# Attention beside a gated mlp on one core: row maxima in visits of four over six banks, and another order of the first transfers

## The chip, the cores and the metric

The kernel runs on one core of a Trainium2 chip. The metric is the device time of one execution in microseconds (us); lower is better. Before the change it is 1117.92 us, the median of three runs (1117.37 to 1118.45).

PE is TensorE (matmuls; PEld its loads of stationary operands), DVE is VectorE, ACT is ScalarE, POOL is GpSimd, SP is SyncE, which here issues most DMAs. PSUM, where matmuls write, has eight banks of 128 x 512 fp32.

## The reference

One input x of 2048 tokens x 448 feeds two branches, which a gate per token mixes: attention with 16 heads of 28, and an mlp behind a layernorm.

```python
def _A_ref(x, wqkv, wo):
    qkv = (x @ wqkv).reshape(B, S, 3, H, Dh).transpose(2, 0, 3, 1, 4)
    q, k, v = qkv[0], qkv[1], qkv[2]
    scores = einsum("bhqd,bhkd->bhqk", q, k) * (Dh ** -0.5)
    o = einsum("bhqk,bhkd->bhqd", softmax(scores), v)
    return o.transpose(0, 2, 1, 3).reshape(B, S, D) @ wo
def _B_ref(x, w1, b1, w2, b2):
    h = gelu(layernorm(x) @ w1 + b1)        # 448 -> 1792
    return h @ w2 + b2                      # 1792 -> 448
g = sigmoid((x * gate_w).sum(-1, keepdims=True))
return g * _A_ref(x, wqkv, wo) + (1 - g) * _B_ref(x, w1, b1, w2, b2)
```

All of it is fp32. The kernel splits operands into a high part that TensorE takes (type fp32r) and the low rest, and adds the products high x high, high x low and low x high: three matmuls for one product.

## The kernel before, in words

**Stages.** (1) The head: q and k of the first 512 tokens, then q, k and v of all tokens, with the layernorm's statistics beside them. (2) The mlp, in four chunks of 512 tokens; for each chunk `mlp1` makes 14 blocks of 128 hidden units (11 matmuls each, L612), and `mlp2` makes four blocks of 128 tokens (14 x 3 matmuls each, L625, L626, L630). (3) Attention: scores, exponentials on ACT, products with v, and the output projection.

**Row maxima.** The softmax needs the maximum of each row of scores ahead of the exponentials. The class `RowMax` finds it with a cheaper product of high parts: one matmul (L440) gives the scores of 128 queries of one head with 512 keys in one bank, and DVE reduces it (L420 for one bank, L422 for two neighbouring banks at once). A head has 28 rows, so four heads lie in the four strips of 32 partitions (`j`), and the heads go round by turns. A block is four heads x 512 queries: 64 such matmuls, and a 65th slot (`close`, L406) that transposes the block's maxima, eight matmuls into the next block. There are 16 blocks, 1040 slots in all. Slot and block order: `left` holds what a block has left, `done` counts slots.

**Visits.** During the mlp these slots are put between its matmuls. After each matmul of the mlp `Filler.run` adds a weight to `slot`; `due` says how many of 482 slots (`MLP_MAX`) should be done by now, spread evenly over the stretch that begins at f = 4 of the first chunk (`FS`, L667), where a matmul of `mlp1` counts 0.65 x 0.233, later 0.233, and one of `mlp2` 0.205 (`W1`, `W2`). Is a visit's worth due (`MG` = 6), then six slots are issued at once, into banks 2 to 7; banks 0 and 1 belong to the mlp. Matmuls run in the order of the program. A matmul into a bank waits until DVE has reduced what stood there; DVE takes its instructions in the order in which they stand. In the attention stage `scores` puts single slots between its own products (banks 5 and 6).

The keys for the row maxima (`khr`, four strips) are loaded by four DMAs on POOL's queue at f = 1 of the first chunk (`load_khr`, L503), the queries (`qd`) on SP's.

**The head.** `WARM` = 8 matmuls of zeros (L276) run first. q and k together have seven blocks of 128 outputs (m), and 448 inputs are laid out as four pieces of 128 rows (t; the last holds 64 rows twice). `turns` gives the order in which weights `("w", m)`, all four t at once, and inputs `("x", t)` of the first 512 tokens are fetched: w0, x0, w1, x1, w2, x2, w3, x3, w4, w5, w6; x0 on ACT's queue, all else on SP's. In the same order ACT makes the high parts (L183, L202), POOL or DVE the low parts (L184, L204), and PE runs every product that has just become possible into seven banks (L322, 77 matmuls), the products with low weights one turn later. After that come the v tiles (L234) and the other q, k tiles (L222).

Of the kernel before, what the change touches and what calls it, by code (L numbers as in the profile page):

```python
# [15 lines left out]
P = 128  # L16
# [16 lines left out]
MG = 6  # L33
FS = 4
WARM = 8
# [7 lines left out]
def kernel(ctx: ExitStack, tc: tile.TileContext, xt, wqk, wv, wo, xk, w1, b1, w2, b2,  # L43
# [114 lines left out]
    with tc.tile_pool(name="qx", bufs=2) as qx, tc.tile_pool(name="qo", bufs=4) as qo, \  # L158
# [15 lines left out]
        wh, wl, wt = {}, {}, {}  # L174

        def fetch_wqk(m):
            wt[m] = halves.pop(0).rearrange("p (t x) -> p t x", t=4)
            nc.sync.dma_start(wt[m], wqk[m])

        def split_wqk(m):  # L180
            wh[m] = qw.tile([P, 4, P], F32R, name=f"wh{m}")
            wl[m] = qw.tile([P, 4, P], F32R, name=f"wl{m}")
            nc.scalar.activation(wh[m], wt[m], AF.Copy)  # L183
            nc.gpsimd.tensor_sub(wl[m], wt[m], wh[m].bitcast(F32))  # L184
# [30 lines left out]
        def qk_tile(c, m):  # L215
            ps = next_ps()
            ops = []
            for t in range(3):
                ops += [(wh[m][:, t], xh[c][:, t]), (wh[m][:, t], xl[c][:, t]), (wl[m][:, t], xh[c][:, t])]
            ops += [(wh[m][:, 3], xh[c][:, 3]), (wl[m][:, 3], xh[c][:, 3])]  # L220
            for i, (a, b) in enumerate(ops):
                nc.tensor.matmul(ps, a, b, start=(i == 0), stop=(i == len(ops) - 1))  # L222
            qk_out(c, m, ps)
# [49 lines left out]
        zeros = spare(NF - 1)[:, 0, :P]  # L273
# [9 lines left out]
        halves = [x[:, i] for n in range(NF // 2, NF - 1) for x in [spare(n)] for i in range(2)]  # L283
        turns = [x for i in range(NM) for x in ([("w", i), ("x", i)] if i < 4 else [("w", i)])]
        for what, i in turns:
            if what == "w":
                fetch_wqk(i)
            else:
                fetch_x(0, i, nc.sync if i else nc.scalar)
# [6 lines left out]
        for v in vt:  # L296
            nc.gpsimd.memset(v[:, :, DH:DH + 1], 1.0)
            nc.gpsimd.memset(v[:, :, DH + 1:32], 0.0)
        banks = [next_ps() for m in range(NM)]
        there, pieces, late, count = [], [], [], [0] * NM  # L300
        for what, i in turns:
            if what == "w":
                if i < 4:
                    split_wqk(i)
                there.append(i)
                new = [(i, t) for t in pieces]
            else:
                split_x(0, i)
                pieces.append(i)
                new = [(m, i) for m in there]  # L310
            ops = [("hh", m, t) for m, t in new]

            low, late = late + [("lh", m, t) for m, t in new], []
            if what == "w":
                late = [x for x in low if x[1] == i]
            ops += [x for x in low if x not in late]
            ops += [("hl", m, t) for m, t in new if t < 3]
            if i == NM - 1:
                ops += late
            for k, m, t in ops:  # L320
                a, b = wl[m] if k == "lh" else wh[m], xl[0] if k == "hl" else xh[0]
                nc.tensor.matmul(banks[m], a[:, t], b[:, t], start=(count[m] == 0), stop=(count[m] == 10))  # L322
                count[m] += 1
                if m == 0 and count[m] == 11:

                    for n in range(4, NM):
                        split_wqk(n)
                    for n in range(4):
                        nc.scalar.activation(wvh[:, n], wvr[n], AF.Copy)
                        nc.gpsimd.tensor_sub(wvl[:, n], wvr[n], wvh[:, n].bitcast(F32))  # L330
# [630 lines left out]
```

## Time and profile before

| what | value |
| --- | --- |
| median of three runs | 1117.92 us |
| the profiled execution's own time | 1117.1 us |
| its span, first to last instruction | 1115.3 us |
| PE busy | 1106.8 us, 99% of the span |
| DVE / ACT / POOL busy | 741.2 / 634.8 / 334.0 us |
| first and last matmul of L322 | 6.36 us, and the first v tile starts at 26.08 us |
| first matmul of the mlp | 116.19 us |
| last visit of the mlp over | 456.98 us |

The profile is one execution. Times are us from the start of the span unless marked ns. In the order of time a row gives start, length, engine, line, operation, what it writes <- reads, the shape and how many equal instructions it joins; in brackets stands the idle time ahead of it and what ended it. In the groups of instructions the columns are the count, the busy time, the mean length in ns, then the idle time ahead and what ended it. Matmuls are pipelined: one starts before the one ahead of it has ended, so their lengths overlap, and a pace is read from starts. In the view of stretches the columns are the window, its length, the busy time of PE, PEld, DVE, ACT and POOL with the number of instructions, the granted clock of PE, the DMA engines' share and GB/s.

### The profile page before, as it was taken

Reading aid. Unit: us, or ns where it says so; the run is one execution under the profiler, and the core shown is the slowest. Engines: PE = TensorE matmul, PEld = TensorE weight load, DVE = VectorE, ACT = ScalarE, POOL = GpSimd, SP = SyncE. Lnnn points to the kernel's source line nnn. Section 1 sums busy time; section 2 is a strip of 40 time slices with the busy share of each in tenths; the row PEclk is TensorE's granted clock in tenths of the full one; section 3 lists DMA queues with packets and bytes.
Section 4 is the critical chain, followed back from the end, with each engine's and each line's share of the span. In section 5 each row is a group of like instructions: output and inputs, shape, how many; then the busy total and the mean of one; then the engine's idle time right before and its main releaser. Section 6 shows DMA issues by size and latency. Waiting matters only on the chain.

```text
span 1115.3 us, 19794 instructions
## 1 busy us (share of the span) xinstructions
PE 1106.8 (99%) x8152; PEld 674.9 (61%) x8152; DVE 741.2 (66%) x1030; ACT 634.8 (57%) x660; POOL 334.0 (30%) x354
## 2 busy tenths in 40 slices
PE   9999999999999999999999999999999999999998
PEld 7888777777777777744444444444444444454546
DVE  4553398988888889576766766666667767746103
ACT  5334651330231232287887887887878878847572
POOL 5016664242344231013112221320223024342350
PEclk9999999999999999999999999999999999999999
DMA  7988641011121023162100220012021003002011
GB/s 247 363 266 284 179 122 53 9 47 36 50 55 37 25 53 87 41 166 79 28 19 20 61 72 19 21 28 52 26 59 37 18 20 94 12 26 69 34 53 58
DMA packets 53079, 84.35 MB, mean 76 GB/s; under 512 B 8516, under 2 KB 28500, under 8 KB 52076
## 3 DMA queue, kind: packets, MB, share of 16 engines
q1 hardware_dynamic: 48588, 76.01, 22.2%
q0 software_dynamic: 4256, 6.81, 2.3%
q8 instruction: 64, 1.05, 0.4%
q10 hardware_dynamic: 144, 0.26, 0.1%
q14 instruction: 27, 0.22, 0.1%
HBM read 56.40 MB, written 26.49 MB: 74 GB/s over the span
## 4 chain that ended last, share of the span: by engine, by line
PE 98%; DVE 1%; ACT 1%; DMA 0%; issue 0%; ACTq 0%
PE bank L828 22%; PE bank L563 20%; PE bank L440 16%; PE bank L612 13%; PE bank L222 5%; PE bank L630 5%; PE bank L625 4%; PE bank L626 4%; PE bank L234 3%; PE bank L322 2%; PE bank L733 1%; PE bank L734 1%; PE bank L735 1%; DMA w1f<-in_wqk 0%; ACT khi L567 0%
## 5 line engine op out<-in xcount | busy, mean ns | idle before, releaser
L567 ACT ACTIVATE pt<-bank 128x1536 f32<-128x1536 f32 (+1 forms) x386 | 460.3, 1243 | 121.7 <-PE bank L563 121.7
L420 DVE TENSOR_REDUCE mx<-bank 128x1 f32<-128x512 f32 x618 | 409.8, 688 | 174.0 <-PE bank L440 160.1
L828 PE MATMUL bank<-pt,vg 128*32 128x512 f32 x1942 | 260.4, 602 | 0.0
L422 DVE TENSOR_REDUCE mx<-bank 128x2 f32<-128x1024 f32 x203 | 238.9, 1220 | 30.3 <-PE bank L440 30.0
L440 PE MATMUL bank<-khi,qd 28*128 28x512 f32 x512 | 241.9, 480 | 0.1
L440 PEld LDWEIGHTS bank<-khi,qd 28*128 28x128 f32 x512 | 92.3, 181 | 148.1 <-DVE mx L420 104.4
L563 PE MATMUL bank<-qh,klo 28*128 28x512 f32 x1024 | 174.2, 394 | 0.0
L563 PE MATMUL bank<-qh,khi 29*128 29x512 f32 x768 | 156.3, 480 | 0.8 <-ACT khi L567 0.6
L612 PE MATMUL bank<-y,w1f 128*128 128x512 f32 x616 | 151.9, 397 | 0.0
L612 PEld LDWEIGHTS bank<-y,w1f 128*128 128x128 f32 x616 | 112.6, 188 | 33.1 <-issue 10.8
L563 PE MATMUL bank<-ql,khi 28*128 28x512 f32 x768 | 128.8, 390 | 0.0
L617 POOL TENSOR_TENSOR hl<-h,hh 128x512 fp32r<-128x512 f32 x56 | 72.5, 1295 | 117.6 <-ACT h L616 77.4
L615 ACT ACTIVATE hh<-bank,b1s 128x512 fp32r<-128x512 f32 x56 | 38.7, 691 | 98.6 <-PE bank L612 98.6
L828 PEld LDWEIGHTS bank<-pt,vg 128*32 128x32 f32 x1942 | 44.6, 108 | 78.7 <-issue 78.3
L563 PEld LDWEIGHTS bank<-qh,klo 28*128 28x128 f32 x1024 | 87.2, 185 | 3.6
L636 ACT ACTIVATE h<-bank 128x448 f32<-128x448 f32 x16 | 8.7, 546 | 137.9 <-PE bank L630 103.6
L749 POOL DMA_DIRECT2D lt<-ob x15 | 10.9, 727 | 253.0 <-DVE ob L748 253.0
L630 PE MATMUL bank<-w2h,hl 128*128 128x448 f32 x224 | 85.0, 379 | 0.0
L563 PEld LDWEIGHTS bank<-qh,khi 29*128 29x128 f32 x768 | 60.6, 181 | 39.8 <-ACT pt L567 25.0
L625 PE MATMUL bank<-w2h,hh 128*128 128x448 f32 x224 | 83.3, 372 | 0.0
L626 PE MATMUL bank<-w2l,hh 128*128 128x448 f32 x224 | 81.9, 366 | 0.0
L440 PE MATMUL bank<-khr,qd 28*128 28x512 f32 x512 | 80.3, 467 | 0.5 <-issue 0.3
(135 smaller groups left out, 1298.0 us busy)
## 6 DMA issues: line engine op xcount, KB each, us to landing
qk<-hl SPq DMA_DIRECT2D x28, 512.0 KB
vs<-vt SPq DMA_DIRECT2D x16, 256.0 KB
s<-in_xt SPq DMA_DIRECT2D x16, 256.0 KB
raw<-in_xt SPq DMA_DIRECT2D x15, 256.0 KB
rc<-rls POOLq DMA_DIRECT2D x60, 64.0 KB, 2.2
w1f<-in_xk SPq DMA_DIRECT2D x8, 448.0 KB
gbs<-h SPq DMA_DIRECT2D x16, 224.0 KB
klo<-qk SPq DMA_DIRECT2D x16, 224.0 KB
```

The lines of the kernel that those rows point to most:

```text
L222: nc.tensor.matmul(ps, a, b, start=(i == 0), stop=(i == len(ops) - 1))
L420: nc.vector.reduce_max(self.mx[:, c0:c0 + 1], bank[:, b0], axis=AX)
L422: nc.vector.reduce_max(self.mx[:, c0:c1 + 1:c1 - c0], bank[:, b0:b1 + 1], axis=AX)
L440: nc.tensor.matmul(bank[:, b], self.qds[self.n][r, i * P:(i + 1) * P], khi[self.n // NC][r, k * 512:(k + 1) * 512], start=True, stop=True)
L563: nc.tensor.matmul(bank[:, p], a[r, k * P:(k + 1) * P], b[r], start=(i == 0), stop=(i == 2))
L567: nc.scalar.activation(t, bank[:, at[0]:at[-1] + 1], AF.Exp, scale=SCALE)
L612: nc.tensor.matmul(ps, a, b, start=(i == 0), stop=(i == len(ops) - 1))
L617: nc.gpsimd.tensor_sub(hl[f], h, hh[f].bitcast(F32))
L625: nc.tensor.matmul(a, hh[f][:, sl], w2h[f], start=(f == 0), stop=False)
L626: nc.tensor.matmul(a, hh[f][:, sl], w2l[f], start=False, stop=False)
L630: nc.tensor.matmul(a, hl[f][:, sl], w2h[f], start=False, stop=(f == NF - 1))
L828: nc.tensor.matmul(pv[32 * j:32 * j + 32, :], vg[n // NC][:, k, 32 * j:32 * j + 32], probs.pop(4 * step + j), start=(k == 0), stop=(k == N ...
```

## The change

Two things are changed, and one constant.

**Visits of four.** `MG` goes from 6 to 4. A visit no longer begins at bank 2: `Filler.turn` goes on by four with each visit, and the slots take banks 2 + (turn + i) mod 6. `issue` takes a list of banks in place of a first one and a count; two banks are reduced together only if they are neighbours. The single slots of the attention stage keep their banks. `MLP_MAX`, the weights and the end of the stretch stay.

**The first transfers.** The weights of q and k are in one tile for all m, and are fetched in pieces: first t = 0 for m = 0 and 1, then x0, then t = 0 for m = 2 to 6, then x1, and after these t = 1 to 3 of each m with x2 and x3 between them. All are on SP's queue. The products follow the new order; those with low weights of t = 1 to 3 are one turn late. The splits of v's weights stand behind the outputs of m = 2 and m = 3, those of the next x pieces behind m = 5 and 6. `WARM` goes from 8 to 9.

```diff
-MG = 6
+MG = 4
-WARM = 8
+WARM = 9
...
+        def fetch_wqk(place, m, t):
+            n, k = m.stop - m.start, t.stop - t.start
+            wt[m.start, t.start] = r = place[:, :n * k * P].rearrange("p (m t x) -> p m t x", m=n, t=k)
+            nc.sync.dma_start(r, wqk[m, :, t].rearrange("m p t x -> p m t x"))
+        def split_wqk(m, t):
+            r = wt.pop((m.start, t.start))
+            nc.scalar.activation(wh[:, m, t], r, AF.Copy)
+            nc.gpsimd.tensor_sub(wl[:, m, t], r, wh[:, m, t].bitcast(F32))
...
-        turns = [x for i in range(NM) for x in ([("w", i), ("x", i)] if i < 4 else [("w", i)])]
-                fetch_x(0, i, nc.sync if i else nc.scalar)
+        one, more3 = slice(0, 1), slice(1, 4)
+        rest = [("w", slice(m, m + 1), more3) for m in range(NM)]
+        turns = [("w", slice(0, 2), one), ("x", 0), ("w", slice(2, NM), one), ("x", 1), *rest[:2], ("x", 2), rest[2],
+                 ("x", 3), *rest[3:]]
+        for what, *a in turns:
+            if what == "x":
+                fetch_x(0, *a)
+            elif a[1] is one:
+                fetch_wqk(whole[:, a[0].start * P:], *a)
             else:
+                fetch_wqk(halves.pop(0), *a)
...
+            ops = [("hh", m, t) for m, t in new] + [("hl", m, t) for m, t in new if t < 3]
+            low = [("lh", m, t) for m, t in new]
+            if what == "w" and a[1] is more3 and a is not turns[-1][1:] and a[0].start < NM - 1:
+                ops, late = ops + late, low
+            else:
+                ops, late = ops + late + low, []
...
                 if count[m] == 11:
+                    if m == 0:
+                        for _, *b in rest[3:]:
+                            split_wqk(*b)
+                            split.add((b[0].start, b[1].start))
                     qk_out(0, m, banks[m])
-                    if m in (1, 3):
-                        split_x(1, m // 2)
-                        fetch_x(1, m // 2 + 2)
+                    for n in {2: (0,), 3: (1, 2, 3)}.get(m, ()):
+                        split_wv(n)
+                    if m in (3, 5):
+                        fetch_x(1, m // 4 + 2)
+                    if m > 4:
+                        split_x(1, m - 5)
...
-        def issue(self, first, n, rows=None):
+        def issue(self, banks, rows=None):
-            for b in range(first, first + n):
+            for b in banks:
-                if held and held[0][1] > at:
+                if held and (held[0][1] > at or held[0][0] + 1 != b):
                     reduce()
...
             if self.max is not None and self.due(n) >= min(MG, self.upto - self.done) > 0:
-                self.max.issue(2, min(MG, self.upto - self.done))
+                self.max.issue([2 + (self.turn + i) % 6 for i in range(min(MG, self.upto - self.done))])
+                self.turn += MG
```

More of the change, by code (lines that the diff above doesn't have):

```diff
@@ L320 @@
             for k, m, t in ops:
-                a, b = wl[m] if k == "lh" else wh[m], xl[0] if k == "hl" else xh[0]
-                nc.tensor.matmul(banks[m], a[:, t], b[:, t], start=(count[m] == 0), stop=(count[m] == 10))
+                w, x = wl if k == "lh" else wh, xl[0] if k == "hl" else xh[0]
+                nc.tensor.matmul(banks[m], w[:, m, t], x[:, t], start=(count[m] == 0), stop=(count[m] == 10))
                 count[m] += 1
[L324 to L330, printed above, removed]
@@ L544, in load_qm @@
         while filler.done < min(65 * NG * NC, 65 * (n + 1) + 9):
-            filler.max.issue(5, 1)
+            filler.max.issue([5])
         g, c = divmod(n, NC)
@@ L573, in scores @@
         if most > 0:
-            filler.max.issue(5, 1, [(units[0] + 3) % 4])
+            filler.max.issue([5], [(units[0] + 3) % 4])
         for i in range(3):
```

62 lines of the change are left out of this document (26 added, 36 removed).

## The prediction

> **What bounds the kernel now.** I read first the page's chain of work that ended last, then the groups of instructions inside the mlp's stretch, then the order of time on PE around single visits of the row maxima, and last the first 26 us.
>
> ```profile
> span 1115.3 us, 19794 instructions
> PE 98%; DVE 1%; ACT 1%; DMA 0%; issue 0%; ACTq 0%
> PE bank L828 22%; PE bank L563 20%; PE bank L440 16%; PE bank L612 13%; PE bank L222 5%; PE bank L630 5%; PE bank L625 4%; PE bank L626 4%; PE bank L234 3%; PE bank L322 2%; PE bank L733 1%; PE bank L734 1%; PE bank L735 1%; DMA w1f<-in_wqk 0%; ACT khi L567 0%
> ```
>
> The last work to end is a chain of PE instructions from end to end. So a microsecond more or less of PE time in any stage is a microsecond in the whole, and the question is what the change does to PE in two places: the mlp (L612, L625, L626, L630, with the visits of L440 between them) and the head (L322). Everything behind the mlp is issued as before: 482 row-maximum slots are done by then in both kernels.
>
> The mlp's stretch from its first matmul to the end of its last visit is 116.19 to 456.98, that is 340.8 us. The groups there:
>
> ```profile
> L612 PE MATMUL bank<-y,w1f 128*128 128x512 f32 x616 | 151.9, 397 | 0.0
> L630 PE MATMUL bank<-w2h,hl 128*128 128x448 f32 x206 | 78.4, 381 | 0.0
> ...
> L440 PE MATMUL bank<-khr,qd 28*128 28x512 f32 x475 | 62.7, 466 | 0.5 <-issue 0.3 <-DVE mx L422 0.2
> L406 PE MATMUL bank<-ident,mf 128*16 128x128 f32 x7 | 1.9, 276 | 0.0
> ```
>
> The mean lengths overlap (PE starts the next matmul before the last has ended), so they can't be added. Starts can. In order of time on PE, columns start, length, line, tile, count:
>
> ```profile
> 116.19 14.93 PE L612 MATMUL bank<-y,w1f 128*128 128x512 f32 x65
> 131.04 0.50 PE L440 MATMUL bank<-khr,qd 28*128 28x512 f32 x3
> 131.84 0.51 PE L440 MATMUL bank<-khr,qd 28*128 28x512 f32 x3 [0.30 <-issue]
> 132.28 4.85 PE L612 MATMUL bank<-y,w1f 128*128 128x512 f32 x20
> ...
> 172.37 0.36 PE L626 MATMUL bank<-w2l,hh 128*128 128x448 f32 x1
> 172.66 0.73 PE L440 MATMUL bank<-khr,qd 28*128 28x512 f32 x6
> 173.33 0.47 PE L630 MATMUL bank<-w2h,hl 128*128 128x448 f32 x1
> 173.64 0.37 PE L625 MATMUL bank<-w2h,hh 128*128 128x448 f32 x1
> 173.84 0.36 PE L626 MATMUL bank<-w2l,hh 128*128 128x448 f32 x1
> ...
> 270.67 0.37 PE L626 MATMUL bank<-w2l,hh 128*128 128x448 f32 x1
> 270.96 0.51 PE L440 MATMUL bank<-khr,qd 28*128 28x512 f32 x4
> 271.40 0.28 PE L406 MATMUL bank<-ident,mf 128*16 128x128 f32 x1
> 271.61 0.49 PE L440 MATMUL bank<-khr,qd 28*128 28x512 f32 x1
> 272.03 0.47 PE L630 MATMUL bank<-w2h,hl 128*128 128x448 f32 x1
> 272.34 0.36 PE L625 MATMUL bank<-w2h,hh 128*128 128x448 f32 x1
> ```
>
> 65 matmuls of L612 take 14.93 with the last one's 0.40, so they start every 0.227; those of mlp2 every 0.203 (173.64 to 173.84 and on). A plain visit of six is the second piece. Four matmuls use the four row strips of 28 partitions and run together; a fifth has to wait for its strip, so six are two rounds. From L626 at 172.37 to L625 at 173.64 are 1.27; without the visit two starts, 0.41. **A visit of six costs 0.86.** Its parts: 0.29 to get in (0.20 without a visit), 0.67 for two rounds, 0.31 to get back to pace.
>
> The third piece shows what one round costs. Four matmuls at 270.96, then a matmul on all 128 rows at 271.40: 0.44. One at 271.61, then L630 at 272.03: 0.42. The first piece has three at 131.84 and L612 at 132.28: 0.44. So a lone round takes 0.44 before a full-height matmul can start, and the second round of a pair adds only 0.67 - 0.44 = 0.23, because its weights were loaded under the first and the emptying of the array is paid once.
>
> **The change, part by part.**
>
> *Visits of four.* A visit is now 0.29 + 0.44 + 0.31 - 0.41 = 0.63 in mlp2; in mlp1 it is much the same, so I take 0.64. 482 slots make 120 visits of four and one of two, where there were 80 of six and one of two: 120 x 0.64 - 80 x 0.864 = 76.8 - 69.1 = **+7.7 us**. Each maximum costs PE 0.16 where it cost 0.144. Bounds by the rows: 0.42 to 0.44 for the round gives 7.7 less 2.4 to 7.7.
>
> The Trainium skill (TensorEngine Tiling (Array Packing), Key Properties) says that a change of tiling mode drains TensorE, which speaks against more and shorter visits; the 0.42 to 0.44 above agree.
>
> *Closing a block of 64.* Seven times a slot of the stretch is the transpose of L406, at slots 72, 137, 202, 267, 332, 397 and 462. It uses all rows, so in the middle of a visit it cuts a round in two: 270.67 to 272.34 are 1.67 less 0.41, that is 1.26, 0.40 above a plain visit. Modulo six four slots fall in the middle and three at an edge: some 1.8 in all (an edge one 0.1 by the same starts). Modulo four they are 0, 1, 2, 3, 0, 1, 2. In the middle: 0.29 + 0.43 + 0.21 + 0.43 + 0.31 - 0.41 = 1.26, now 0.62 above plain, four times; with the three others some 2.9. **+1.1**.
>
> *The first visit.* `due` lets a visit go when as many are due as it takes. By lines 667 and 483 each matmul of the first mlp1 adds 0.65 x 0.233 x 482 / 248.5 = 0.294, so six are due with the 21st matmul of f = 4 (44 + 21 = the 65 above), four with the 14th: 7 x 0.227 = 1.6 sooner, at 129.45. The keys' rows come on POOL's queue at line 503:
>
> ```profile
> L503 POOL DMA_DIRECT2D khr<-qk x4: 511/520/764, 121.5 to 123.2; - x4
> ...
> DMA to landing us min/median/max: 6.5/7.4/8.5
> ```
>
> The fourth strip lands at 123.2 + 8.5 = 131.7, which is why the first visit of before is split: three at 131.04, the rest at 131.84, which cost it 0.57 over a plain one. Now PE stands from 129.45 until 131.84, 2.4. Behind the waiting matmul on PE is the whole mlp, and nothing else can start it. **+1.8**; it would be 0 if the landing moved forward with it, but the DMAs are issued from the same place in the code, so it doesn't.
>
> *Six banks by turns.* Before, a visit took all six banks and its second round the two banks that DVE reads last; now the next visit begins on two banks that were read a visit ago. DVE's groups in the mlp:
>
> ```profile
> L422 DVE TENSOR_REDUCE mx<-bank 128x2 f32<-128x1024 f32 x203 | 238.9, 1220 | 30.3 <-PE bank L440 30.0
> ...
> L420 DVE TENSOR_REDUCE mx<-bank 128x1 f32<-128x512 f32 x69 | 47.2, 684 | 7.7 <-PE bank L440 7.6
> ...
> PEld bank L440 <- DVE mx L422: 6.7, 19, 0.5
> ...
> 173.20 3.49 DVE L422 TENSOR_REDUCE mx<-bank 128x2 f32<-128x1024 f32 x3 [0.42 <-PE bank L440]
> ```
>
> PE waited for DVE at 19 weight loads (part of that is the drain). What the waits cost is what is left of the stretch: 340.8 - 616 x 0.227 - 618 x 0.203 (L625 and L626 stand in the loop of L630, three times 206) = 75.5 for all visits; less 69.1, 1.8, 0.57 and 0.64 for the visit of two leaves 3.4. The order of the changed program has 185 reductions of two banks and 105 of one in place of 203 and 69, since a pair now breaks at a visit's edge in every second block. Back to back a pair takes 3.49 / 3 = 1.16 and a single 0.7 at most: at worst 1.16 + 1.4 = 2.6 a visit, and visits come every 2.7 (a block's four, 10 x 0.203 + 0.64). It holds, and a late reduction now has a bank in hand. I leave 0.7 of the 3.4: **-2.7** (bounds -3.4, and +1 should DVE fall behind).
>
> *The head.* Rows of PE, ACT and of the stretches (columns there: PE, PEld, DVE, ACT, POOL busy, clock, DMA share, GB/s):
>
> ```profile
> 1.20 3.78 PE L276 MATMUL bank<-w1f 128*128 128x128 f32 x16 [1.20 <-DVE w1f L274]
> 6.36 0.79 PE L322 MATMUL bank<-xh,wh 128*128 128x512 f32 x1 [1.37 <-ACT xh L202]
> ...
> 8.76 0.63 PE L322 MATMUL bank<-xl,wh 128*128 128x512 f32 x1
> 9.19 1.01 PE L322 MATMUL bank<-xh,wh 128*128 128x512 f32 x2
> 10.04 0.86 PE L322 MATMUL bank<-xh,wl 128*128 128x512 f32 x3
> ...
> 26.08 0.36 PE L234 MATMUL bank<-wvh,xh 128*128 128x450 f32 x1
> ...
> 5.15 0.63 ACT L183 ACTIVATE wh<-w1f 128x512 fp32r<-128x512 f32 x1 [2.71 <-DMA w1f<-in_wqk]
> 5.69 0.61 ACT L202 ACTIVATE xh<-raw 128x512 fp32r<-128x512 f32 x1
> ...
> 2.00:4.00 2.00, 2.00 (x11) 2.00 (x11) 0.00 (x0) 0.44 (x1) 0.00 (x0) 1.00 0.78 196
> 4.00:5.00 1.00, 0.98 (x5) 0.69 (x4) 0.00 (x0) 0.00 (x0) 0.00 (x0) 1.00 0.87 256
> 5.00:6.30 1.30, 0.00 (x0) 0.00 (x0) 0.00 (x0) 1.15 (x3) 0.44 (x1) 1.00 1.05 403
> ```
>
> Warm-up ends at 4.98, the first real matmul waits until 6.36 for two transfers of 262 KB (w of m = 0, x of t = 0), seven matmuls, 0.43 apart and more, fill the time until 10.04, and then 70 take 16.05, 0.229 each without a gap. The granted clock reads 1.00 all along; the half pace is to be seen in the starts alone. Seventy-seven at 0.229 are 17.7, the head has 26.08 - 6.36 = 19.7.
>
> Now PE needs 131 + 262 KB first. At 196 GB/s from 2 us on 393 KB are in at 3.9 (36 KB before 2 us), 524 KB at about 4.4; ACT began 0.75 after that, and 0.67 lie between xh's start and the matmul: 3.9 + 0.75 + 0.67 = 5.3. The ninth warm-up adds two records of 0.22 and ends at 5.4, so PE goes on without a gap at 5.4, 0.95 sooner. Later transfers (0.33 MB for m = 2 to 6, then x of t = 1) are ahead of the 21 matmuls of t = 0. If the pace is full soon after 5.4, with 0.3 for the first xl, the head ends at 23.4, 2.7 sooner; if it stays half until 10.04 as before, 11 matmuls go by then and 66 x 0.229 end at 25.2, 0.9 sooner. I take **-2.0**, nearer to the first, since the half pace of before began anew after a gap that is closed now. The other end: if one queue gets only half of the 196 that two shared, 393 KB are in at 5.6 and the first matmul at 7.1: +0.7. POOL's and ACT's splits of wv come later than before, behind the outputs of m = 2 and 3; by my count the last wvl is ready at 24, and its first use is the tenth matmul of the v tile. Without that cover a v tile would wait 1 us.
>
> The Trainium skill (TensorE: Matmul & The Clock Gate, Part 1) has the array at half clock until a free-running window of 3.4 us was busy. With PE busy from 1.20 on the full pace would then begin between 4.6 and 8.0, and the head's gain, by an estimate from that page, be 1.5 to 2.7; the trace of before, half pace for 3.7 us after the gap, agrees.
>
> **Sum.** 7.7 + 1.1 + 1.8 - 2.7 - 2.0 = +5.9. The profiled execution took 1117.1 (span 1115.3, 1.8 around it), so 1123.0; it lies 0.8 below the median of the runs, 1117.92, and against that I say **1123.8**.
>
> **Rivals.**
>
> *A, faster: the lone round leaves as quickly as a second one.* The second round of 172.66 lets L630 in 0.33 after its own start. Were that so for a round of four, a visit costs 0.53, 120 of them 63.6, 5.5 less than now; with the other terms (+1.1 + 1.8 - 2.7 - 2.0) -7.3: 1110.6. It decides from a round of about 0.39 down, where the sum is nil. For it: the same banks and strips; against it: three rows of 0.42 to 0.44, one with exactly four. A tenth.
> The skill's span model (the page on the clock gate, Part 3) counts one matmul and some 4 ns a tile and no price for the switch; by that alone four would be best. That the four of 270.96 end within 0.51, where the one of 271.61 takes 0.49, agrees; the emptying that the rows show isn't in it.
>
> *B: DVE sets the pace.* With 36 more single reductions, PE waits in the broken blocks as now, 3.4, and 0.1 more in each of some 42 visits: 2.7 + 4.2 above my sum, 1130.7. For it: 2.6 of 2.7 at the longest lengths; against it: the bank in hand. 0.08.
>
> *C: the head gains nothing*, as one queue is slower while it starts: +0.7 in place of -2.0, 1126.5. For it: 196 GB/s with two queues; against it: 403 as soon as one was left. 0.12.
>
> **How the numbers follow.** My forecast has 0.7, from 1121 to 1126 by its bounds (the head 0.7 better or 1.1 worse, DVE 0.7 better or 1.5 worse, the round's 0.42). The range takes in C and leaves out A and B, 0.18 together: 1120.0 to 1128.5. Two executions differ by about 0.2%, 2.2 us, without a cause. Faster is A, 0.10; within 0.2% what lies between A and the forecast's low end, 0.05; slower the rest, 0.85.
>
> **What would show it.** Visits of `x4` on PE, from the row ahead to the second row behind 1.04, and 0.44 from `x4` to the next L612 or L625 to L630; 121 visits and 348 to 350 us for the stretch of the mlp; the first visit split, its last matmul 2.4 behind its first; waits for L422 under half; first L322 at about 5.4 and first L234 near 24. The forecast is wrong if the row behind `x4` starts 0.33 after it, if the mlp's stretch is not longer, or if later stages, which the change doesn't touch, take another time.

## The result, and the profile after

| kernel | median, us | lowest to highest | runs |
| --- | --- | --- | --- |
| before | 1117.66 | 1117.36 to 1118.45 | 6 |
| after | 1124.58 | 1123.48 to 1125.96 | 6 |

The ratio after to before is 1.0062, with a 95% interval of 1.0049 to 1.0075. The changed kernel is slower by 6.9 us, where the prediction said 5.9 (1123.8). The profiled execution of after took 1124.77, with a span of 1123.0; that of before had 1115.3, so 7.7 us have to be found in the two traces.

The page of after, with its span and its chain of work that ended last:

```profile
span 1123.0 us, 19831 instructions
PE 97%; DMA 1%; DVE 1%; ACT 1%; issue 0%; POOL 0%; SPq 0%; POOLq 0%; ACTq 0%
```

PE is the bound as before. Lines have moved with the diff: L612 is now L629 (mlp1), L625, L626 and L630 are L642, L643 and L647 (mlp2), L440 is L456 (the maxima), L406 is L422 (the transpose at a close), L420 and L422 are L436 and L438 (DVE's reductions), L322 is L337 (the head), L222 and L234 are L225 and L237 (q,k and v), L276 is L280 (warm-up).

Order of time on PE in the mlp of after, columns start, length, line, tiles, count:

```profile
114.94 1.32 PE L629 MATMUL bank<-y,w1f 128*128 128x512 f32 x5
...
128.20 0.50 PE L456 MATMUL bank<-khr,qd 28*128 28x512 f32 x2
129.56 0.50 PE L456 MATMUL bank<-khr,qd 28*128 28x512 f32 x1 [0.85 <-DMA khr<-qk]
131.08 0.47 PE L456 MATMUL bank<-khr,qd 28*128 28x512 f32 x1 [1.03 <-issue]
131.48 2.79 PE L629 MATMUL bank<-y,w1f 128*128 128x512 f32 x11
...
162.65 0.37 PE L643 MATMUL bank<-w2l,hh 128*128 128x448 f32 x1
162.95 0.50 PE L456 MATMUL bank<-khr,qd 28*128 28x512 f32 x4
163.38 0.48 PE L647 MATMUL bank<-w2h,hl 128*128 128x448 f32 x1
163.70 0.37 PE L642 MATMUL bank<-w2h,hh 128*128 128x448 f32 x1
...
231.65 0.84 PE L629 MATMUL bank<-y,w1f 128*128 128x512 f32 x3
232.42 0.50 PE L456 MATMUL bank<-khr,qd 28*128 28x512 f32 x1
232.84 0.28 PE L422 MATMUL bank<-ident,mf 128*16 128x128 f32 x1
233.05 0.50 PE L456 MATMUL bank<-khr,qd 28*128 28x512 f32 x2
233.48 0.73 PE L629 MATMUL bank<-y,w1f 128*128 128x512 f32 x2
...
463.88 0.50 PE L456 MATMUL bank<-khr,qd 28*128 28x512 f32 x2
464.31 0.47 PE L642 MATMUL bank<-w2h,hh 128*128 128x448 f32 x1
```

- The stretch from the first matmul of the mlp to the end of its last visit is 114.94 to 464.31, 349.4 us, where before had 340.8: +8.6.
- A plain visit: from L643 at 162.65 to L642 at 163.70 are 1.05, less 0.41 for two starts is 0.64. From the four at 162.95 to L647 are 0.43.
- A close in the middle, read from the visit's first matmul: L422 comes 0.42 behind it, the second round 0.63 and L629 1.06. The whole visit costs 1.26.
- The first visit has its four matmuls at 128.20, 128.20, 129.56 and 131.08, as the key strips land one after the other.

Over all 121 visits, taken in the same way from the row ahead to the second row behind, PE loses 82.65 us to visits, the middle one 0.638. Before it was 74.52 for 81 visits, the middle one 0.865.

DVE's groups and the weight loads of the maxima in the same stretch of after:

```profile
L438 DVE TENSOR_REDUCE mx<-bank 128x2 f32<-128x1024 f32 x184 | 219.2, 1220 | 33.2 <-PE bank L456 31.4
L436 DVE TENSOR_REDUCE mx<-bank 128x1 f32<-128x512 f32 x105 | 69.5, 683 | 9.0 <-PE bank L456 8.8
L456 PEld LDWEIGHTS bank<-khr,qd 28*128 28x128 f32 x475 | 24.2, 181 | 43.0 <-issue 31.5 <-DVE mx L436 5.1 <-DVE mx L438 3.4
```

The idle time behind the bar says less than it seems: the weight loads still stood 8.5 us behind a reduction (5.1 + 3.4), and yet no plain visit of after but the first costs more than 0.06 above the middle one. Before, ten plain visits did, by 1.45 together, beside smaller ones.

The head of after, PE, ACT and the stretches (columns as in the prediction):

```profile
1.20 4.21 PE L280 MATMUL bank<-w1f 128*128 128x128 f32 x18 [1.20 <-DVE w1f L278]
6.31 1.22 PE L337 MATMUL bank<-xh,wh 128*128 128x512 f32 x2 [0.91 <-ACT xh L205]
...
9.04 2.06 PE L337 MATMUL bank<-xh,wh 128*128 128x512 f32 x5
10.94 1.32 PE L337 MATMUL bank<-xl,wh 128*128 128x512 f32 x5
...
25.93 0.36 PE L237 MATMUL bank<-wvh,xh 128*128 128x450 f32 x1
...
3.00 0.42 ACT L186 ACTIVATE wh<-w1f 128x256 fp32r<-128x256 f32 x1 [1.00 <-DMA w1f<-in_wqk]
5.63 0.63 ACT L205 ACTIVATE xh<-raw 128x512 fp32r<-128x512 f32 x1 [2.21 <-DMA raw<-in_xt]
...
2.00:4.00 2.00, 2.00 (x11) 2.00 (x11) 0.00 (x0) 0.42 (x2) 0.50 (x1) 1.00 0.87 154
```

The weights are there at 3.0, but x lands only for 5.63, and the first matmul starts at 6.31, not at 5.4; between 2 and 4 us the DMAs moved 154 GB/s. Five matmuls at 9.04 still take 1.90 to the next row, 0.38 each; the five at 10.94 are at full pace. The head ends at 25.93, 0.15 sooner than before.

The rest of the ledger, by starts: q, k and v, from the first v matmul to the mlp, took 116.19 - 26.08 = 90.11 and now 114.94 - 25.93 = 89.01, so **-1.1**, which the prediction doesn't have. What follows the last matmul of the mlp took 0.4 longer (469.63 to the end of 1115.3; 476.96 to the end of 1123.0). Together 8.6 - 0.15 - 1.1 + 0.4 = 7.7, within rounding.

### The profile page after: what moved, and what is told of

The parts are those of the page before. It is cut to its first block, busy times and chain, and to the rows that moved or that the text cites. A ratio compares the mean times of both kernels' runs of the same rounds, so it can differ in the third digit from the quotient of the medians.

```text
span 1123.0 us, 19831 instructions
## 1 busy us (share of the span) xinstructions
PE 1113.4 (99%) x8154; PEld 667.4 (59%) x8154; DVE 743.6 (66%) x1048; ACT 633.7 (56%) x662; POOL 332.3 (30%) x356
## 3 DMA queue, kind: packets, MB, share of 16 engines
q8 instruction: 64, 1.05, 0.4%
## 4 chain that ended last, share of the span: by engine, by line
PE 97%; DMA 1%; DVE 1%; ACT 1%; issue 0%; POOL 0%; SPq 0%; POOLq 0%; ACTq 0%
PE bank L845 22%; PE bank L580 20%; PE bank L456 15%; PE bank L629 13%; PE bank L647 5%; PE bank L225 5%; PE bank L642 4%; PE bank L643 4%; PE bank L237 3%; PE bank L337 2%; PE bank L750 1%; PE bank L751 1%; PE bank L752 1%; DMA khr<-qk 1%; DMA raw<-in_xt 0%
## 5 line engine op out<-in xcount | busy, mean ns | idle before, releaser
L436 DVE TENSOR_REDUCE mx<-bank 128x1 f32<-128x512 f32 x654 | 431.8, 686 | 175.0 <-PE bank L456 160.8
L438 DVE TENSOR_REDUCE mx<-bank 128x2 f32<-128x1024 f32 x185 | 220.4, 1220 | 33.2 <-PE bank L456 31.4
L456 PE MATMUL bank<-khi,qd 28*128 28x512 f32 x512 | 241.7, 479 | 0.2
L456 PEld LDWEIGHTS bank<-khi,qd 28*128 28x128 f32 x512 | 92.3, 181 | 148.6 <-DVE mx L436 107.3
L629 PE MATMUL bank<-y,w1f 128*128 128x512 f32 x616 | 158.2, 402 | 0.0
L629 PEld LDWEIGHTS bank<-y,w1f 128*128 128x128 f32 x616 | 111.1, 188 | 35.5 <-issue 14.5
L647 PE MATMUL bank<-w2h,hl 128*128 128x448 f32 x224 | 86.1, 384 | 0.0
L642 PE MATMUL bank<-w2h,hh 128*128 128x448 f32 x224 | 84.2, 376 | 0.0
L456 PE MATMUL bank<-khr,qd 28*128 28x512 f32 x512 | 81.7, 493 | 1.9 <-issue 1.0
L643 PE MATMUL bank<-w2l,hh 128*128 128x448 f32 x224 | 81.9, 366 | 0.0
```

Of the source, the lines that this page charges most:

```text
L436: nc.vector.reduce_max(self.mx[:, c0:c0 + 1], bank[:, b0], axis=AX)
L438: nc.vector.reduce_max(self.mx[:, c0:c1 + 1:c1 - c0], bank[:, b0:b1 + 1], axis=AX)
L456: nc.tensor.matmul(bank[:, b], self.qds[self.n][r, i * P:(i + 1) * P], khi[self.n // NC][r, k * 512:(k + 1) * 512], start=True, stop=True)
L642: nc.tensor.matmul(a, hh[f][:, sl], w2h[f], start=(f == 0), stop=False)
L643: nc.tensor.matmul(a, hh[f][:, sl], w2l[f], start=False, stop=False)
L647: nc.tensor.matmul(a, hl[f][:, sl], w2h[f], start=False, stop=(f == NF - 1))
```

## The experiments

### The two parts, each alone

`visits_alone` is the kernel before with the visits of after and the old head; `head_alone` is after with visits of six.

```diff
 visits_alone, against before
-MG = 6
+MG = 4
...
-                self.max.issue(2, min(MG, self.upto - self.done))
+                self.max.issue([2 + (self.turn + i) % 6 for i in range(min(MG, self.upto - self.done))])
+                self.turn += MG
 head_alone, against after
-MG = 4
+MG = 6
```

> The kernel before with visits of four over six banks by turns, head as before. Theory (each visit pays one emptying of the array, 0.64 us for four against 0.865 for six): the mlp's visits cost 82.6 us in place of 74.5, time 1117.7 + 8.1 to 8.6 = 1126, ratio 1.0075. Rival (the mlp's longer stretch comes from the shifted head or from other work beside it): within 0.2% of before, 1116 to 1120.

> The changed kernel with visits of six (always banks 2 to 7, since six by turns is the same six), new head kept. Theory: mlp as before (visits 74.5 us, first visit split once), the gain of the head's part alone, 1.2 us: 1116.4, ratio 0.9989. By my prediction's head term it would be 1115.7. Rival (the new head itself costs time further on): 1118 or more.

`visits_alone`: 1127.12 (1125.42 to 1127.19), ratio 1.0076 (1.0063 to 1.0089), the kernel before on the same chip 1117.84. `head_alone`: 1116.31 (1113.86 to 1117.62), ratio 0.9981 (0.9972 to 0.9990). The visits alone cost more than the whole change, and the head with its new weight tile gives 1.5 us. In the trace of `visits_alone` 121 visits sum to 81.8 us, and the mlp is 9.3 longer than before. So the loss is the visits', and with these medians the parts add up to 9.3 - 1.5 = 7.8, where the whole change has 6.9.

Of the 9.3 in the mlp only 7.3 lie in the visits (81.8 - 74.5), and most of the rest stands right behind the first one. The order of time on PE in `visits_alone` (its L613 is mlp1), and the stretch behind it with the granted clock as its sixth figure behind the length:

```profile
130.46 0.47 PE L440 MATMUL bank<-khr,qd 28*128 28x512 f32 x1 [0.85 <-DVE mx L422]
130.85 5.07 PE L613 MATMUL bank<-y,w1f 128*128 128x512 f32 x14
...
131.00:134.50 3.50, 3.50 (x11) 2.75 (x12) 1.72 (x2) 0.65 (x2) 1.22 (x1) 0.62 0.72 225
```

and in a second profile of after (`second_look`, below):

```profile
130.07 0.47 PE L456 MATMUL bank<-khr,qd 28*128 28x512 f32 x1 [1.03 <-DVE mx L438]
130.47 3.51 PE L629 MATMUL bank<-y,w1f 128*128 128x512 f32 x14
```

The same fourteen matmuls take 5.07 and 3.51: in the first kernel eight of them start 0.43 apart, for 3.4 us, and that costs 1.6. Here the granted clock shows it, 0.62 over the stretch, and over the whole run as a mean of 0.998. The half pace follows the waits of the first visit in some executions and not in others: of six profiles with visits of four and keys at f = 1, four show it (`visits_alone`, and below `fixed_banks`, `warm_up_12`, `x0_on_act`), the two of after don't, and of the other eight profiles none has it at this place. So the first visit has a second price behind it, of 1.6 in part of the executions; what decides between them stays open. How often after pays it can't be counted: over its six runs its mean clock is 1.0 twice and 0.997 to 0.998 four times, but a mean doesn't say where the clock fell. The 0.998 of `one_weight_tile` (below) comes from its head, and six of fifteen runs of before beside `visits_alone` have 0.998, too. The Trainium skill (TensorE: Matmul & The Clock Gate, Part 1) has the clock fall after an idle window of some 3.4 us. That the half pace lasts 3.4 us agrees with its window; that PE must stand idle for so long doesn't, since the wait in the row above is 0.85 and matmuls run between the waits of this visit. (The brackets of both rows name a reduction; the fourth strip of the keys landed at 130.36 and 129.98, 0.1 ahead of them.)

### Is it the round, or the number of maxima?

If the round is the unit, a fifth maximum opens a second round and a visit of five costs as much as one of six. If a visit costs a fixed part and one for each maximum, it lies halfway between four and six, 0.75.

```diff
-MG = 4
+MG = 5
```

> The changed kernel with visits of five. Theory (rounds: five need two rounds, as six do): 96 visits at 0.865 = 83.2 us against 120 at 0.638 = 76.6, so 6 us slower than four: about 1130. Rival (a price per visit and one per matmul, on a line through four and six: 0.18 + 0.114 a matmul, 0.75 for five): 96 x 0.75 = 72, between four and six: about 1120.

1127.04 (1126.99 to 1127.30), ratio 1.0080 (1.0065 to 1.0094). The order of time on PE in this kernel:

```profile
172.09 0.36 PE L643 MATMUL bank<-w2l,hh 128*128 128x448 f32 x1
172.39 0.73 PE L456 MATMUL bank<-khr,qd 28*128 28x512 f32 x5
173.05 0.47 PE L647 MATMUL bank<-w2h,hl 128*128 128x448 f32 x1
173.36 0.37 PE L642 MATMUL bank<-w2h,hh 128*128 128x448 f32 x1
```

From 172.09 to 173.36 are 1.27, the same as for the six of the prediction's rows, and from the five to L647 are 0.66. Over 97 visits the middle one is 0.859. The linear rival falls: a visit costs 0.64 with one round and 0.86 with two, and five slots are the worst use of two. The time lies 3 us under the expected 1130: the first visit, due later, costs 1.9 in place of 3.5, and in its profile the head ends 1.84 sooner than in that of after (24.09).

### What the six banks by turns are worth

```diff
-                self.max.issue([2 + (self.turn + i) % 6 for i in range(min(MG, self.upto - self.done))])
+                self.max.issue([2 + i for i in range(min(MG, self.upto - self.done))])
```

> The changed kernel with every visit of four in banks 2 to 5. Theory (the turns take the waits for VectorE away): a visit comes 2.7 us after the one before, VectorE is through with its second pair 2.9 us after that one began, so most visits wait 0.2 us and split their round (0.2 to 0.4 more): 90 visits x 0.3 = 27, time 1140 to 1155. Rival (rotation isn't what removed the waits, fewer banks per visit is enough): 1124 to 1127.

1146.95 (1145.25 and 1148.66), ratio 1.0260 (1.0238 to 1.0283). One of its visits in the order of time on PE:

```profile
165.39 0.50 PE L456 MATMUL bank<-khr,qd 28*128 28x512 f32 x2
166.41 0.50 PE L456 MATMUL bank<-khr,qd 28*128 28x512 f32 x2 [0.53 <-DVE mx L438]
166.84 0.48 PE L647 MATMUL bank<-w2h,hl 128*128 128x448 f32 x1
```

The second pair has to wait until DVE has read its banks from the visit before, so one round becomes two with a gap. Sixty of the visits of four without a transpose cost over 0.06 more than 0.638, 22.2 us together (the first visit's 2.9 among them), and all visits sum to 102.8. In after the same sum is 82.65. So the turns are worth 20 us to visits of four: by turns each visit finds its banks read.

### The first visit and its keys

The keys of the first maxima are fetched (L520, POOL's queue) at f = 1 of the mlp. This kernel fetches them at f = 0.

```diff
-                    if f == 1:
+                    if f == 0:
```

> The changed kernel, with the four DMAs of the row maxima's keys issued one block of the mlp sooner (f = 0 in place of f = 1). Theory: the first visit no longer waits for the fourth strip, 3.48 us becomes 0.64 to 1.3, time 2.2 to 2.8 lower: 1122. Rival (the landing follows other traffic, or the visit waits for the queries instead): the first visit still over 2 us, 1124 to 1125.

1122.00 (1121.29 to 1122.31), ratio 1.0033 (1.0020 to 1.0046), 2.6 less than after and the time that was expected. But the way isn't the expected one. PE and ACT of this kernel, in order of time:

```profile
118.65 4.47 PE L629 MATMUL bank<-y,w1f 128*128 128x512 f32 x19
125.23 0.96 PE L629 MATMUL bank<-y,w1f 128*128 128x512 f32 x3 [2.11 <-ACT h L633]
...
128.62 0.50 PE L456 MATMUL bank<-khr,qd 28*128 28x512 f32 x4
129.06 3.45 PE L629 MATMUL bank<-y,w1f 128*128 128x512 f32 x14
...
122.92 0.63 ACT L106 ACTIVATE w1f<-more 128x512 fp32r<-128x512 f32 x1 [3.44 <-DMA more<-in_w]
```

The first visit is whole now, with 0.44 to the next matmul, and costs 0.63 where after's cost 3.48. All that it had above a plain one, 2.84, was the wait for the keys. Yet 2.28 of them come back earlier: PE stands until 125.23 for a bank that ACT has not read, and ACT's queue stands until 122.92 behind the split of a weight block (L106), whose transfer is late; in after that split came at 121.36 without a wait. All three versions with the keys at f = 0 have such a stop at this place (2.3 here, 1.4 and 1.5 in the two below), and none of the eleven other profiles has one, so moving the keys brings it. That the keys' own transfer is what delays the other one is likely, but was not tried by itself. The mlp is 361.57 long, after's 362.02 and 361.55: the wait has moved. In the profiles (spans of 1120.5 and 1123.0) 2.0 of the gain on after is a head that ends sooner, which the keys don't touch, and 0.45 is the mlp. That the sooner keys also spare the half pace behind the first visit would fit the mean clock (1.0 in all four runs, in after in two of six), but isn't shown. So of the 2.6 little is shown to be the keys'.

### The head: warm-up, queue, and the same kernel again

Three runs ask why the head gave less than foreseen. `warm_up_12` has `WARM = 12` in place of 9, to close the gap in front of the first matmul. `x0_on_act` puts the first x back on ACT's queue. `second_look` is after itself with a new profile.

```diff
 warm_up_12
-WARM = 9
+WARM = 12
 x0_on_act
-                fetch_x(0, *a)
+                fetch_x(0, *a, queue=nc.sync if a[0] else nc.scalar)
```

> The changed kernel with 12 warm-up matmuls in place of 9, so that the gap ahead of the first real matmul (5.4 to 6.3 us in its profile) is closed. Theory (full pace needs an unbroken stretch of work, by a window whose phase changes from run to run): the half pace ends before 8 us in every run, the head ends at 23.5 to 24.5, time 0.5 to 1.5 lower than the changed kernel and closer together. Rival (the half pace ends at a time that gaps don't set): no change, 1124 to 1125.

> The changed kernel, with the transfer of x for the first 128 inputs issued from ACT again, beside the queue of SP. If one queue is what makes x land late (split of x starts at 5.1 to 5.9 where the prediction had 4.6), x starts at 4.6 or before, the first matmul moves to about 5.4 and the run gains 0.3 to 0.8 on the changed kernel. If the transfers' own slow stretch at 3 to 4.5 us is the cause, x starts between 5.1 and 5.9 as with one queue and the time is the same within 0.5.

> The changed kernel itself, once more, with a new profile. Question: whether the head's end at 25.93 in its first profile is typical. Theory (the head's half pace ends at a time that varies from execution to execution, and mostly early): first v matmul near 24.0, mlp start near 113.0, mlp length 362 again, profiled execution about 1122.8, median of the runs 1122.5 to 1124.6. Rival (visits of four somehow make the head end late): 25.9 again, mlp start 114.9 and 1124.6.

`warm_up_12`: 1123.67 (1123.10 to 1124.85), ratio 1.0050 (1.0037 to 1.0063); its interval and that of after overlap, so a gain isn't shown. The gap isn't quite closed: the warm-up ends at 5.85 and the first matmul starts at 6.17. But its warm-up shows when the full pace comes: the records start every 0.213 until 4.8 and every 0.112 from then on, and the head ends at 24.04, as was expected. `x0_on_act`: 1125.93 (1123.80 to 1127.22), ratio 1.0069 (1.0055 to 1.0083), which overlaps with after, too. `second_look`: 1124.43 (1122.15 to 1127.65), ratio 1.0064 (1.0047 to 1.0081); its head ends at 25.43, so the late end of the first profile was no exception among the runs of after, and the expected 24.0 was missed.

In `x0_on_act` the split of the weights starts at 5.33, 2.3 later than in after, that of x right behind it at 5.66, and the first matmul at 6.32, with two queues as with one:

```profile
5.33 0.42 ACT L186 ACTIVATE wh<-w1f 128x256 fp32r<-128x256 f32 x1 [2.87 <-DMA w1f<-in_wqk]
5.66 0.61 ACT L205 ACTIVATE xh<-raw 128x512 fp32r<-128x512 f32 x1
...
2.00:4.00 2.00, 2.00 (x11) 2.00 (x11) 0.00 (x0) 0.46 (x1) 0.00 (x0) 1.00 0.80 151
```

So a second queue brings the first matmul no sooner: the later of the two transfers that it needs is in between 5.3 and 5.7 in either form, and between 2 and 4 us both forms move about 150 GB/s. When x itself landed here can't be read, since ACT was still waiting for the weights. Why the transfers are slow there stays open.

How long a new head takes from its first matmul to the first v matmul falls in two groups. Rows of the version with visits of six and sooner keys (the last but one below), which is in the other group than after:

```profile
5.81 0.84 PE L337 MATMUL bank<-xh,wh 128*128 128x512 f32 x2 [0.40 <-ACT xh L205]
...
7.57 1.30 PE L337 MATMUL bank<-xh,wh 128*128 128x512 f32 x5
8.70 1.29 PE L337 MATMUL bank<-xl,wh 128*128 128x512 f32 x5
...
23.66 0.36 PE L237 MATMUL bank<-wvh,xh 128*128 128x450 f32 x1
```

Here five matmuls take 1.13 from 7.57 on, full pace, and the head lasts 17.85. Of ten profiles with the new head eight last 17.85 to 18.0; the one start at 0.39 to 0.50 among their first matmuls waits for DVE's low part of x (or, here, is the first one), and no stretch of half pace is left in them. The two of after last 19.6 and 19.3, with ten and eight matmuls at 0.39 to 0.59 to the next, most at 0.43. `keys_sooner`, `fixed_banks`, `visits_of_five` and `head_alone` have the same head as after and are in the faster group, so neither the code of the head nor visits of four put after into the slower one; why both its profiles are there stays open. (One run of `second_look` at a mean clock of 1.0 took 1122.15, 1.6 less than its profiled 1123.74, which would fit a fast head; no trace shows it.) With the old head they are 18.7, 19.7, 19.7 and 20.1. The granted clock reads 1.00 in all these heads but the last, that of `one_weight_tile`:

```profile
8.00:10.00 2.00, 2.00 (x6) 1.52 (x6) 2.00 (x2) 1.86 (x4) 2.00 (x2) 0.50 1.05 403
```

There the stretch of half pace is in the record; why it isn't in that of the others stays open.

The Trainium skill (TensorE: Matmul & The Clock Gate, Part 1) says that the window which decides on the full clock runs freely, so that the same kernel can show 6, 11 or 14 slow matmuls. The none, 8 and 10 here, with one and the same head, agree with that; where the window stood in each execution no trace shows.

### The pace of q, k: one weight tile, or where it lies?

The 1.1 us of the q, k stage were unforeseen. Their source can be the single tile for all weights or the place where it lies. `one_weight_tile` is the kernel before with each of wh, wl in one tile; `weights_64_bytes_on` is the kernel before with its fourteen tiles and 64 unused bytes ahead of them; `all_64_bytes_on` is the last version below with 64 unused bytes behind the constants, so that weights and x move together.

```diff
 one_weight_tile, against before
+        wh = qw.tile([P, NM, 4, P], F32R, name="wh")
+        wl = qw.tile([P, NM, 4, P], F32R, name="wl")
-        wh, wl, wt = {}, {}, {}
+        wh, wl, wt = [wh[:, m] for m in range(NM)], [wl[:, m] for m in range(NM)], {}
...
-            wh[m] = qw.tile([P, 4, P], F32R, name=f"wh{m}")
-            wl[m] = qw.tile([P, 4, P], F32R, name=f"wl{m}")
 weights_64_bytes_on, against before
         mr = qw.tile([P, 2, NT], F32, name="mr")
+        pad = qw.tile([P, 16], F32, name="pad")
 all_64_bytes_on, against six_keys_sooner
     one_t = const.tile([S // P, P], F32, name="one_t")
+    pad = const.tile([P, 16], F32, name="pad")
```

> The kernel before, with the weights of q and k in one tile each for high and low, in place of seven; nothing else. Theory (the place of the weights in memory sets the pace of the q and k matmuls): they start every 0.227 us as in the changed kernel, in place of 0.232, 231 matmuls give 1.1 us, time 1116.6. Rival (the pace follows from what else runs beside them, transfers or splits, which the new head orders otherwise): pace 0.231 to 0.233, time 1117.7.

> The kernel before with 64 unused bytes a partition laid ahead of the weights of q and k, which stay fourteen tiles; nothing else changes, and the weights begin 64 bytes further on, at the same place modulo 128 as in the changed kernel. If the pace of the q,k matmuls (0.2317 before, 0.2269 with one weight tile) hangs on where the stationary operand lies, it is 0.227 here, the stage from first v matmul to the mlp takes 89.0 in place of 90.1 and the run some 1 us less than before (1116.7). If it hangs on there being one tile (how many waits or semaphores the matmuls carry), it stays at 0.2317 and 90.1, 1117.7.

> The version with visits of six and sooner keys, with 64 unused bytes a partition behind the constants, so that everything of that side lies 64 bytes further on: weights and x of the q,k matmuls both begin at 96 modulo 128 (in the kernel before 96 and 32, in the changed one 32 and 32), and the probabilities of the attention at 96 like the values (32 and 96 until now). Theory 1 (a matmul is slower where its two operands differ by 64 modulo 128): q,k stay at 0.227 and 89.0, and the first of a run of four column tiles with the probabilities (0.433 from start to start) falls towards the later ones' 0.409, at most 2 to 6 us over the attention, so 1109 to 1113. Theory 2 (a stationary operand at 96 modulo 128 is slower by itself): q,k go back to 0.2317 and 90.1, the attention stays, 1115.9. Against theory 2 speak the mlp's first matmuls, 0.227 with both operands at 96.

A run of 77 matmuls of q, k with nothing between, its first and its last, in the kernel before:

```profile
35.12 0.40 PE L222 MATMUL bank<-xh,wh 128*128 128x512 f32 x1
...
52.85 0.39 PE L222 MATMUL bank<-xh,wl 128*128 128x512 f32 x1
```

and in `weights_64_bytes_on`:

```profile
35.21 0.40 PE L222 MATMUL bank<-xh,wh 128*128 128x512 f32 x1
...
52.45 0.39 PE L222 MATMUL bank<-xh,wl 128*128 128x512 f32 x1
```

and in `all_64_bytes_on`:

```profile
33.36 0.40 PE L226 MATMUL bank<-xh,wh 128*128 128x512 f32 x1
...
50.59 0.39 PE L226 MATMUL bank<-xh,wl 128*128 128x512 f32 x1
```

Seventy-six starts take 17.73, 17.24 and 17.23: 0.2333, 0.2268 and 0.2267 each. In `one_weight_tile` it is 0.2268 too, and its stage 89.01, as in after. So 64 unused bytes do it without the single tile. In the programs' layouts the weights begin at 96 modulo 128 bytes before, x at 32; in `weights_64_bytes_on` and in after both at 32, in `all_64_bytes_on` both at 96. Theory 1 holds for these matmuls (slower where the two operands differ by 64 modulo 128; another modulus wasn't tried), and theory 2 falls, since weights at 96 are fast there. For the attention's column tiles theory 1 falls: from start to start they kept 0.433 and 0.409, and the time stayed at 1115.07 (1114.08 to 1117.25), ratio 0.9973 (0.9960 to 0.9985), where 1109 to 1113 was expected. In the whole time the pad alone is at the edge of what the runs can tell: `weights_64_bytes_on` 1116.96 (1115.00 to 1118.99), ratio 0.9990 (0.9979 to 1.0001), and `one_weight_tile` 1117.15 (1115.26 to 1121.39), ratio 0.9997 (0.9985 to 1.0009).

### A version faster than both

The new head and weight tile, the banks by turns, the keys at f = 0, and visits of six:

```diff
-MG = 4
+MG = 6
-                    if f == 1:
+                    if f == 0:
```

> The changed kernel with visits of six and the keys' DMAs one block sooner: the new head, no lone rounds, no wait at the first visit. Theory: head_alone (1116.3) less the 1.4 us that its first visit waits: 1114.9, faster than both kernels. Rival (DMAs issued sooner delay others): 1116 or more.

1114.85 (1114.59 to 1116.95), ratio 0.9978 (0.9969 to 0.9987), 3.0 less than before beside it (1117.81), as expected. Its first visit costs 0.864 and its visits 73.99, but again a stop of 1.41 in mlp1 (for ACT, as above) takes the place of the first visit's wait: the mlp lasts 354.57, in `head_alone` 354.58. The intervals of the two overlap, so the sooner keys aren't shown to help with visits of six; the gain on before is the head's and the weights' place.

## Why the prediction was right, and where it was off

*Visits of four*, +7.7: right. 0.638 each against 0.865, so 120 x 0.638 - 80 x 0.865 = +7.4. A lone round leaves after 0.43 in after's rows, and the visit of five shows that rounds are what is paid. Rival A, whose sum was nil at a round of 0.39, falls.

*Closes*, +1.1: right. The seven visits with a transpose cost 0.74 to 0.75 where it comes first, 1.26 to 1.27 in the middle and 0.66 at the end; over plain ones 2.75 where it was 1.84 before, +0.9.

*The first visit*, +1.8: the mechanism was right, the size too small. It went at 128.20, since the mlp began 1.25 sooner, while the last strip let its matmul go at 131.08, only 0.76 sooner than before. A wait of 2.9 in place of 2.4; +2.3 net, and in four of six profiles another 1.6 behind it, for the half pace that follows the wait there. The latter the prediction didn't have; the profile of after doesn't have it either.

*Six banks by turns*, -2.7: right. Waits on DVE cost the visits of before 2.3 (what its 74.52 has over plain visits, closes and the first) and those of after nothing: -2.4. The prediction had 3.4 for these waits, of which about 0.9 is the pace of mlp1 (0.2286, where it took 0.227), and left 0.7 of them; that it came so near owes something to these two. The sign for it was wrong: waits for L422 were to be under half, and they went from 6.7 to 3.4, with those for the single reductions from 2.1 to 5.1. The sum of these waits stayed; their price didn't. Rival B falls: with 105 single reductions DVE kept up.

In the profile of after these four sum to 7.4 + 0.9 + 2.3 - 2.4 = +8.2 where the prediction had +7.9; the stretch of the mlp was foreseen at 348 to 350 and is 349.4. The remaining 0.4 of its +8.6 lies in the pace of mlp1 between visits (L629 every 0.2298, L612 every 0.2286).

*The head*, -2.0: here the step failed that has the first matmul at 5.4. It took the two queues' 196 GB/s for the single one and x in at 3.9; 154 were moved, x was split at 5.63, and in ten profiles with the new head the first matmul came at 5.8 to 6.6. The other half, that the head then runs 0.227 to 0.229 each, was right in eight of them: 17.9 from the first matmul on, ends at 23.7 to 24.4, 1.7 to 2.4 sooner than before. In both profiles of after the half pace lasted three to four us more, and the term was -0.15 and -0.65. Of the 1.85 that is missing in the first of them, 0.91 is the later first matmul, and 0.94 the pace behind it (19.6 to the first v matmul, where the forecast left 18.7). The premise that the half pace of before began anew after its gap isn't in the rows: its warm-up starts every 0.213 to the end, the pace that `warm_up_12` has ahead of its change to 0.112. Rival C (no gain, +0.7) lies nearer to -0.15 than the forecast and as far from -0.65; its mechanism isn't borne out, since a second queue brought nothing.

*The q, k stage*, unchanged in the prediction: -1.1, from where the weight tile lies. This was not among the terms at all, and it hid part of the smaller gain of the head: -0.15 - 1.1 = -1.25 stands where -2.0 was foreseen, and most of it has another reason.

*Behind the mlp*, nothing foreseen: +0.4 in this pair of profiles. It seems to go with the visits: from the last matmul of the mlp to the end were 645.4 to 645.7 in the seven profiles with visits of five or six, and 645.8 to 646.1 in six with visits of four (647.8 in the seventh, `x0_on_act`). Why stays open.

So the forecast of slower stands on steps that the runs bear out, all of them in the mlp; that the total came within a microsecond owes something to two errors of opposite sign in what comes ahead of it.

## What to carry to other kernels

Where short matmuls of another tiling are put between full-height ones, count rounds, not matmuls: one round cost 0.64 here and two 0.86, so visits of two well-filled rounds are cheaper than twice as many of one, and a fifth slot in a second round is the dearest. (Visits of eight, two full rounds, were not run; the kernel has six banks for them.) A visit that goes sooner needs its operands sooner, and a wait there can also cost pace behind it; but whoever moves that transfer has to look at what it moves back, as a wait of 2.8 us returned as 2.3 elsewhere. And compare the pace of equal matmuls between stages and kernels: 3% can be 64 bytes of layout.

## What the runs showed of the hardware

- The pace of fp32r matmuls of 128 x 128 by 512 columns was 0.2333 with the stationary operand at 96 and the moving one at 32 modulo 128 bytes, and 0.2267 to 0.2268 with both at 32 or both at 96. The Trainium skill (TensorE: Matmul & The Clock Gate, Part 2, Step-by-step) has two independent read ports, so that loading weights takes nothing from the running matmul; from that one would not expect the layout to matter, and the rows show that here it does. Only these three of the four pairings were run, and no trace shows what takes the time.
- With one and the same head the half pace of the start was over ahead of the first product in some executions, and lasted eight or ten products in others. In `warm_up_12` the warm-up shows the change, from 0.213 to 0.112 between records at 4.8 us. The granted clock of the profile read 1.00 there, and 0.50 in one old head (`one_weight_tile`), so that it can't be relied on for the head; the starts can.
- A first visit that waits two or three times within some 2 to 3.5 us, never longer than 1.3 at once, is followed by 3.4 us of half pace in four profiles of six, at a price of 1.6 us each time; a single stop of 2.1 in `keys_sooner` is not. In the four the granted clock tells of it, 0.62 in `visits_alone` from 131 to 134.5.
- Idle time that the trace puts at weight loads behind DVE (8.5 us in after's mlp) cost PE nothing that can be found in the starts.
